# Retention, feed-forward and who issues the output stores: from SyncE to ScalarE, one unit later

## The chip, the cores and the metric

The kernel runs on one core of a Trainium2 chip. The metric is the device time of one execution in microseconds (us). The engines are TensorE (PE in the profile; PEld is its weight load), VectorE (DVE), ScalarE (ACT), GpSimd (POOL) and SyncE (SP); each works through its own list of instructions in order. SP computes nothing here: it issues DMAs. Engines wait for each other, and for DMAs, through semaphores.

## The reference

There are 8 batches of 8 heads, with 576 positions and a head dimension of 64. The first part is a retention layer: scores without a softmax, weighted by a power of a decay that each head has of its own. Its output is laid out as 4608 tokens of 512 values, and goes through a feed-forward layer of width 2048 with a sigmoid-approximated Gelu.

```python
scores = q @ k.T / sqrt(64)                       # each batch and head, 576 x 576
Dmat   = gamma[h] ** (i - j) if i >= j else 0     # gamma[h] = 1 - 2 ** (-5 - h)
ret    = (scores * Dmat) @ v                      # 576 x 64
x      = ret.transpose(0, 2, 1, 3).reshape(4608, 512)
h      = x @ w_in                                 # 512 -> 2048
out    = (h * sigmoid(1.702 * h)) @ w_out         # 2048 -> 512, float32
```

## The kernel before

**Two streams in one order.** The feed-forward layer is done in nine *chunks* of 512 tokens. `hidden` (L723) is one *unit* of its first half: four matmuls of 128x512 into a PSUM bank, and on ACT the Gelu from the bank to `gT` (L734). `project` (L759) is a unit of its second half: four of the sixteen matmuls that make 128 output rows. A chunk has four such *rows*, r = 0 to 3, of four units each (g = 0 to 3); rows 0 to 2 run interleaved, and row 3 after them (in chunk 0 all four are interleaved; chunk 1 is done in two halves, with rows 0 and 1 after the first and rows 2 and 3 after the second). When g is 3 a row is complete: ACT (in the last chunk DVE) copies the bank into one of three buffers `osb` (L771, L774), and SP issues the store to the output (L777, 256 KB). The buffer is chosen by a counter of the rows modulo 3.

Between these units lie the *steps* of retention for the later batches (`step`, `burst`): short 64x64 matmuls (L596 to L638), with DVE for masks, sums and the copy into `xT`. Which step comes behind which unit is written out by hand, in dictionaries that `run` (L953) reads. All of the units' banks come from three that take turns (`next_bank`), so a unit's matmuls wait until ACT has emptied the bank of three units ago.

**Transfers.** POOL issues the loads of q, k and v, three batches ahead, with at most a few in flight. SP issues the DMA transposes (`turn_dma`, L530) that turn the loaded q and k into `qk`, and, in the same list, the stores. SP's list follows the order in which the program was written down.

**Waits.** `Rec` records every operation and works out its waits: a reader waits for the last writer of a tile, a writer for the readers, DMAs among them. An engine waits for its own earlier operations too, except on PE and SP. A copy into an `osb` buffer thus waits for the landing of the store that last read this buffer.

**`later`.** This list holds operations that are recorded after the next unit. In the kernel before it holds only casts that ACT does for some of the steps (L717): `run` empties it behind each unit.

```python
unit(ahead)
while later:
    later.pop(0)()
```

The functions that the change touches, and what calls them:

Of the kernel before, what the change touches and what calls it, by code (L numbers as in the profile page):

```python
# [131 lines left out]
def bass_retnet_parallel__then__act_gelu_quick_kernel(  # L132
# [9 lines left out]
    R = Rec()  # L142
    es = ExitStack()
    with es:
        def sb(name, shape, dtype):
            return es.enter_context(nc.sbuf_tensor(name, shape, dtype))
# [33 lines left out]
        osb = [sb(f"osb{i}", [P, 512], FP32) for i in range(3)]  # L180
# [392 lines left out]
        def needs(m_out, m_in):  # L573
            r = []
            if m_out is not None:
                b, cs = chunks(m_out)
                r += [("sm", si(m_out)), "zw"] + [("v", b % NST, c) for c in cs] + queries(m_out)
            if m_in is not None:
                b, cs = chunks(m_in)
                r += [(nm, b % NST, c) for nm in "kv" for c in cs]  # L580
                r += [("qk", (NC * b + c) % NQK, 1) for c in cs] + queries(m_in)
            return r
# [113 lines left out]
        later = []  # L696
# [62 lines left out]
        def project(c, r, g, bank, key, eng="DVE", ahead=()):  # L759
            def fn(e):  # L760
                for f in range(4 * g, 4 * g + 4):
                    i = e.matmul(bank, gT[c % 2][:, f, 128 * r : 128 * r + 128], w_out_sb[:, f, :],  # L762
                                 start=(f == 0), stop=(f == NF - 1))
                return i
            R.op("PE", fn, r=[("w_out", g)] + [("gT", c % 2, f) for f in range(4 * g, 4 * g + 4)]
                 + list(ahead), ps=[key])
            if g == 3:
                m = ocount[0] % 3
                ocount[0] += 1
                if eng == "ACT":  # L770
                    R.op("ACT", lambda e: e.activation(osb[m].ap(), bank, AF.Copy),  # L771
                         w=[("osb", m)], ps=[key])
                else:
                    R.op("DVE", lambda e: e.tensor_copy(osb[m].ap(), bank),  # L774
                         w=[("osb", m)], ps=[key])
                row0 = 512 * c + 128 * r
                R.op("SP", lambda e: e.dma_start(out[row0 : row0 + 128, :], osb[m].ap()),  # L777
                     r=[("osb", m)], dma=("osb", m))

        def project_pieces(c, r, banks):  # L780

# [171 lines left out]
        def run(units, between):  # L953
            for i, unit in enumerate(units):
                ahead = []
                for fn, *args in between.get(i, ()):
                    if fn is step:
                        ahead += needs(args[0], args[0] + 1 if (len(args) < 2 or args[1])
                                       and args[0] + 1 < NWIDE else None)
                unit(ahead)  # L960
                while later:
                    later.pop(0)()
                for fn, *args in between.get(i, ()):
                    fn(*args)

# [7 lines left out]
        def units_o(c, rows, eng="ACT"):  # L973
            banks = {}

            def unit(r, g):
                def go(ahead):
                    if g == 0:
                        banks[r] = next_bank()
                    project(c, r, g, *banks[r], eng=eng, ahead=ahead)  # L980
                return go
            first = rows[:3]
            return ([unit(r, g) for g in range(4) for r in first]
                    + [unit(r, g) for r in rows[3:] for g in range(4)])

        first = {r: next_bank() for r in (1, 2, 3)}
        first[0] = wide_banks[3]
        run([lambda ahead, r=r, g=g: project(0, r, g, *first[r], eng="ACT", ahead=ahead)
             for g in range(4) for r in range(4)],
            {1: [(tail_turn,)], 3: [(intra, 4)], 5: [(turn, 5), (tail_out,), (regroup, 2)],  # L990
             7: [(scale_v, 5), (turn, 6)], 8: [(scale_v, 6), (regroup, 3)], 9: [(burst, None, 0, "ACT")],
             12: [(turn, 7)], 13: [(step, 0, False)], 14: [(scale_v, 7)], 15: [(turn, 8)]})
        turn_step(3)
        turn_step(4)
        run(units_half(1, 0),
            {0: [(turn, 9, True), (scale_v, 8), (scale_v, 9)], 1: [(burst, None, 1, "ACT")],
             5: [(step, 1)]})
        run(units_o(1, (0, 1)), {3: [(scale, 3)], 5: [(step, 2, False)]})
        run(units_half(1, 1), {2: [(burst, None, 3, "ACT")], 4: [(scale, 4)]})
        run(units_o(1, (2, 3)), {0: [(step, 3, True, "ACT")], 5: [(step, 4, False)], 6: [(scale, 5)]})  # L1000
# [19 lines left out]
        for r in range(3):  # L1020
            bank = next_bank()
            for g in range(4):
                project(NCH - 1, r, g, *bank)
# [59 lines left out]
```

## Time and profile before

| | |
|---|---|
| time, median of 3 runs | 300.65 us (299.34 to 302.87) |
| the profiled execution: its time | 299.83 us |
| its span in the profile | 298.0 us |
| PE busy | 290.4 us, 97% of the span |
| ACT busy | 125.8 us, 42% |
| DVE busy | 123.2 us, 41% |
| POOL busy (issue of loads) | 151.2 us, 51% |
| output stores issued by SP | 35 of 256 KB, one of 192 KB, one of 64 KB |
| DMA transposes issued by SP | 60 |
| time from issue to landing, median | store of 256 KB 3.6 us; transposes 7.3 and 7.4 us |

The profile shows one execution. The span is the time from its first instruction to its last; the execution's own time is 1.8 us longer. Busy time is what an engine spent on instructions, without those that only issue DMAs or wait. A wait is put down to the event that came last by the profile; where the engine named had long been done, it was another. "L771" is a line of the kernel.

### The profile page before, as it was taken

The page shows a single profiled execution, that of the slowest core. Times are in us where ns is not written, and L with a number is a line of the kernel's source. Part 1 is how long each engine was busy: PE and PEld are TensorE (multiplying, and loading weights), DVE is VectorE, ACT ScalarE, POOL GpSimd, SP SyncE. Part 2 cuts the span into 40 slices and gives each one's busy share as a digit, 9 for nine tenths or more (in the row PEclk, how much of TensorE's full clock was granted, in tenths as well). Part 3 has the DMA queues.
Part 4 walks back from the last instruction along what each step waited for, and adds up shares of the span by engine and source line. Part 5 has one row for each costly group of instructions (what it writes and reads, how often), then busy time and mean ns, then how long its engine had stood idle before and what let it go on. Part 6 is the DMA issues. An engine that isn't in the chain of part 4 may idle for free.

```text
span 298.0 us, 7691 instructions
## 1 busy us (share of the span) xinstructions
PE 290.4 (97%) x3396; PEld 148.2 (50%) x3396; DVE 123.2 (41%) x221; ACT 125.8 (42%) x208; POOL 151.2 (51%) x204
## 2 busy tenths in 40 slices
PE   7799999999899999999999999999999999999996
PEld 2554456848445444544454444444444444444444
DVE  6879375544435445533506223255226504000012
ACT  6667327617146413550365046503660265026600
POOL 8967969988959777568986896000000000000000
PEclk9999999999999999999999999999999999999999
DMA  9999999999999999999999999904820200030012
GB/s 131 166 194 186 170 171 165 169 137 139 188 142 129 175 155 168 178 127 137 164 213 137 119 186 180 62 2 107 162 46 2 108 35 2 0 108 35 0 47 96
DMA packets 154322, 36.04 MB, mean 121 GB/s; under 512 B 145456, under 2 KB 149808, under 8 KB 154288
## 3 DMA queue, kind: packets, MB, share of 16 engines
q0 software_dynamic: 115776, 18.10, 97.6%
q1 hardware_dynamic: 38512, 17.44, 31.9%
q8 instruction: 27, 0.44, 0.6%
q14 instruction: 7, 0.06, 0.1%
HBM read 36.70 MB, written 9.44 MB: 155 GB/s over the span
## 4 chain that ended last, share of the span: by engine, by line
PE 76%; DMA 10%; POOL 8%; DVE 4%; issue 1%; SPq 0%
PE psH L762 22%; PE psH L729 22%; PE psU L762 12%; PE psU L729 11%; DMA st_q<-in_q_dram 4%; POOL st_k L229 3%; POOL st_v L229 3%; DMA st_k<-in_k_dram 3%; DMA qk<-st_k 2%; PE psA L624 2%; POOL st_q L216 2%; DMA gT<-in_v_dram 2%; PE psA L596 1%; PE psA L638 1%; PE psA L612 1%; PE psA L788 1%
## 5 line engine op out<-in xcount | busy, mean ns | idle before, releaser
L762 PE MATMUL psH<-w_out_sb,gT 128*128 128x512 bf16 x352 | 84.1, 379 | 0.0
L729 PE MATMUL psH<-xT,w_in_sb 128*128 128x512 bf16 x328 | 78.5, 379 | 0.0
L682 DVE TENSOR_TENSOR xT<-psA,gq 128x768 bf16<-128x768 f32 x21 | 20.1, 958 | 117.3 <-PE psA L612 117.3
L734 ACT ACTIVATE gT<-psH 128x512 bf16<-128x512 f32 x82 | 48.8, 597 | 26.1 <-PE psH L729 26.0
L229 POOL DMA_DIRECT2D st_k<-in_k_dram x70 | 52.4, 774 | 13.8 <-DMA st_k<-in_k_dram 9.4
L229 POOL DMA_DIRECT2D st_v<-in_v_dram x70 | 52.1, 770 | 7.4 <-DMA st_v<-in_v_dram 3.5
L762 PEld LDWEIGHTS psH<-w_out_sb,gT 128*128 128x128 bf16 x352 | 33.6, 98 | 39.3 <-DVE sm L693 0.2
L729 PEld LDWEIGHTS psH<-xT,w_in_sb 128*128 128x128 bf16 x328 | 31.7, 98 | 37.7 <-ACT gT L846 0.3
L762 PE MATMUL psU<-w_out_sb,gT 128*128 128x512 bf16 x192 | 47.9, 379 | 1.3 <-DMA qk<-st_k 1.3
L729 PE MATMUL psU<-xT,w_in_sb 128*128 128x512 bf16 x164 | 42.1, 379 | 0.0
L216 POOL DMA_DIRECT2D st_q<-in_q_dram x39 | 35.1, 901 | 10.2 <-DMA st_q<-in_q_dram 8.6
L771 ACT ACTIVATE osb<-psH 128x512 f32<-128x512 f32 x20 | 11.9, 597 | 58.5 <-PE psH L762 58.5
L734 ACT ACTIVATE gT<-psU 128x512 bf16<-128x512 f32 x41 | 24.5, 598 | 12.2 <-PE psU L729 12.2
L762 PEld LDWEIGHTS psU<-w_out_sb,gT 128*128 128x128 bf16 x192 | 18.1, 98 | 22.4 <-issue 1.6
L729 PEld LDWEIGHTS psU<-xT,w_in_sb 128*128 128x128 bf16 x164 | 15.7, 98 | 18.8 <-ACT osb L771 0.3
L387 DVE TENSOR_TENSOR st_v<-st_v,vfac 128x512 bf16<-128x512 bf16 x36 | 23.4, 683 | 3.5 <-DMA st_v<-in_v_dram 3.5
L711 DVE TENSOR_TENSOR zacc<-zacc,psA 128x256 f32<-128x256 f32 x49 | 20.5, 418 | 5.5 <-PE psA L624 4.2
L771 ACT ACTIVATE osb<-psU 128x512 f32<-128x512 f32 x11 | 6.6, 597 | 32.0 <-PE psU L762 28.3
L693 DVE TENSOR_TENSOR sm<-psA,maskw 128x768 bf16<-128x768 f32 x21 | 19.9, 948 | 0.0
L596 PE MATMUL psA<-sm,st_v 64*64 64x64 bf16 x504 | 11.7, 195 | 0.3
L746 PE MATMUL psH<-xT,w_in_sb 128*128 128x256 bf16 x96 | 11.8, 273 | 0.0
L624 PE MATMUL psA<-st_v,st_k 64*64 64x64 bf16 x448 | 11.7, 199 | 0.0
(118 smaller groups left out, 217.9 us busy)
## 6 DMA issues: line engine op xcount, KB each, us to landing
out_dram<-osb SPq DMA_DIRECT2D x35, 256.0 KB, 3.6
st_q<-in_q_dram POOLq DMA_DIRECT2D x31, 128.0 KB, 7.4
st_k<-in_k_dram POOLq DMA_DIRECT2D x57, 64.0 KB, 7.4
st_v<-in_v_dram POOLq DMA_DIRECT2D x57, 64.0 KB, 7.4
w_in_sb<-in_moe_w_in_dram POOLq DMA_DIRECT2D x4, 512.0 KB, 7.5
w_out_sb<-in_moe_w_out_dram POOLq DMA_DIRECT2D x4, 512.0 KB, 11.7
st_k<-in_k_dram POOLq DMA_DIRECT2D x4, 128.0 KB, 4.6
st_q<-in_q_dram POOLq DMA_DIRECT2D x8, 64.0 KB, 7.2
```

The costliest lines, as they stand in the source:

```text
L216: paced(R.op("POOL", lambda e, d=d, s=s: e.dma_start(d, s), w=[(nm, sl, c)], dma=(nm, sl, c), own=pace()))
L229: paced(R.op("POOL", lambda e: [e.dma_start(d, s) for d, s in parts], w=[(nm, sl, c)], dma=(nm, sl, c), parts=2, own=pace()))
L387: R.op(eng, lambda e: e.tensor_tensor(t, t, f, ALU.mult), r=[("vfac", min(b, 1))], w=[("v", sl, c)])
L596: i = e.matmul(psA[half(t), 2 + u, at : at + 64], rows_of(st_v, m_out, g, u, 4 * u + 2 * t + j), smw[si(m_out)][half(r), j, 2 * blk + t, : ...
L624: i = e.matmul(psA[half(j), bank, off + 64 * t : off + 64 * t + 64], rows_of(st_k, m_in, g, u, h), rows_of(st_v, m_in, g, u, h), start=(t ...
L682: R.op("DVE", lambda e: e.tensor_tensor(xT[:, :, t0 : t0 + 192].rearrange("p (u j) n -> p u j n", u=2), psA[:, 2:4, 0:384].rearrange("p u ...
L693: R.op("DVE", lambda e: e.tensor_tensor(o, i, k, ALU.mult), r=["maskw"], w=[("sm", si(m))], ps=["S"])
L711: R.op("DVE", lambda e, to=to, src=src, was=was: e.tensor_tensor(to, was, src, ALU.add), r=[("zacc", (blk - 1) % 3)], w=[("zacc", blk)], p ...
L729: i = e.matmul(bank, w_in_sb[:, a, 128 * f : 128 * f + 128], xT[:, a, 512 * c : 512 * c + 512], start=(a == 0), stop=(a == 3))
L734: R.op("ACT", lambda e: e.activation(gT[c % 2][:, f, :], bank, AF.Gelu_apprx_sigmoid), w=[("gT", c % 2, f)], ps=[key])
L762: i = e.matmul(bank, gT[c % 2][:, f, 128 * r : 128 * r + 128], w_out_sb[:, f, :], start=(f == 0), stop=(f == NF - 1))
L771: R.op("ACT", lambda e: e.activation(osb[m].ap(), bank, AF.Copy), w=[("osb", m)], ps=[key])
```

## The change

ScalarE issues the store of each row that it copied. The store is not recorded at once but put into `later`, and `run` now takes what was in the list *before* the unit and records it behind the unit: a store follows its copy by one unit. (The casts in the list keep their places, since they are put there between units.) The rows of the last chunk, which DVE copies, are stored by SP as before. SP's list keeps the 60 transposes, the two loads of the start and the five stores of the last chunk.

```diff
                 row0 = 512 * c + 128 * r
-                R.op("SP", lambda e: e.dma_start(out[row0 : row0 + 128, :], osb[m].ap()),
-                     r=[("osb", m)], dma=("osb", m))
+
+                def store(by):
+                    R.op(by, lambda e: e.dma_start(out[row0 : row0 + 128, :], osb[m].ap()),
+                         r=[("osb", m)], dma=("osb", m))
+                if eng == "ACT":
+                    later.append(lambda: store("ACT"))
+                else:
+                    store("SP")
...
+                due = list(later)
+                later.clear()
                 unit(ahead)
-                while later:
-                    later.pop(0)()
+                for fn in due:
+                    fn()
                 for fn, *args in between.get(i, ()):
                     fn(*args)
```

In ACT's list the order at the end of a usual chunk becomes: copy of row 0, copy of row 1, store of row 0, copy of row 2, stores of rows 1 and 2, copy of row 3; then the first Gelu of the next chunk, the store of row 3, and the second Gelu. In SP's list the transposes stand behind each other, and 21 of them have a wait for PE added (that the `qk` buffer has been read), which the stores ahead of them had implied.

## The prediction

> **What bounds the kernel now.** I read the page's table of engines first, then its slices, then the waits of TensorE (PE).
>
> ```profile
> span 298.0 us, 7691 instructions
> ...
> PE 290.4 (97%) x3396; PEld 148.2 (50%) x3396; DVE 123.2 (41%) x221; ACT 125.8 (42%) x208; POOL 151.2 (51%) x204
> ...
> PEclk9999999999999999999999999999999999999999
> ```
>
> PE is busy for 290.4 of 298.0 us at a full granted clock, and no other engine is near it. The list of waits, asked for PE alone from 20 us to the end, has one row:
>
> ```profile
> engine line waited for: us in total, times, longest us
> PE psU L762 <- DMA qk<-st_k: 1.3, 1, 1.3
> ```
>
> So after the start-up there is one visible wait of 1.3 us. That is nearly all that a better order of stores could win; a loss has no such limit. The chain from 60 to 78 us tells where it comes from:
>
> ```profile
> 60.46 7.99 DMA st_k<-in_k_dram
> 68.45 0.02 issue
> 68.46 7.38 DMA qk<-st_k
> 75.84 0.24 issue
> 76.09 1.02 PE psU L762 x4
> ```
>
> A load of K lands at 68.45, SP then issues a transpose of it, this lands at 75.84, and PE goes on. The transpose waited for the load, not for a store ahead of it on SP.
>
> **What the change removes.** SP loses 32 of its 37 stores (the copies of L771: 20 + 11 + 1). One takes SP 333 ns (median of L777; 332 to 1145), 10.7 us in all. SP also waited 138.5 us at these stores for the copies (the waits of SP: L777 <- ACT osb L771), with transposes queued behind. Those are issued earlier now, as soon as their loads are there and PE has read the old contents of their buffers. Gain: nothing, since PE waits for a transpose once and that one waited for its load. The bounds are 0 and the 1.3 us of that wait.
>
> **What it adds: issue time on ScalarE (ACT).** 32 x 0.333 = 10.7 us, and ACT's busy time goes from 125.8 to about 136.5 us. What hides it? The place with work close behind a store is the start of a chunk, where the last row's store follows the first Gelu (ACT's timeline, then PE's: start us, us, engine, line, operation, idle before it and what ended that):
>
> ```profile
> 207.80 0.60 ACT L771 ACTIVATE osb<-psU 128x512 f32<-128x512 f32 x1 [2.86 <-PE psU L762]
> 208.66 0.60 ACT L734 ACTIVATE gT<-psH 128x512 bf16<-128x512 f32 x1 [0.27 <-PE psH L729]
> 209.53 0.60 ACT L734 ACTIVATE gT<-psH 128x512 bf16<-128x512 f32 x1 [0.27 <-PE psH L729]
> ```
>
> ```profile
> 210.19 1.89 PE L729 MATMUL psH<-xT,w_in_sb 128*128 128x512 bf16 x8
> ```
>
> Three banks take turns. The Gelu at 209.53 ends at 210.13 and PE needs its bank one unit (0.86 us) after 210.19, at 211.05: 0.92 us spare. With the 0.27 us that ACT idles ahead of it, a store may take 1.19 us before PE notices. The median is 0.33 and the longest of L777 1.145, so I cost this at nothing. Without that cover a store costs what it takes beyond 1.19 us: if it also had to sit out SP's longest transpose issue (2.64 us, L530), 2.64 + 0.33 - 1.19 = 1.8 us, at nine places (row 3 of seven full chunks, and two of chunk 1, done in halves). A store's wait for its own copy is on the same engine a unit back: nothing.
>
> **What it moves: the store of row 0 comes later, and row 3 needs its buffer.** There are three osb buffers and four rows, so the copy of a chunk's row 3 must wait until the store of row 0 has landed; ACT runs in order, so it now stands there with the Gelus behind it. SP issued that store right behind the copy. ACT issues it behind the *copy of row 1*. The kernel before already shows the wait in chunk 2 (again ACT's timeline, then PE's):
>
> ```profile
> 110.32 0.60 ACT L771 ACTIVATE osb<-psU 128x512 f32<-128x512 f32 x1 [9.03 <-PE psU L762]
> 111.19 0.60 ACT L771 ACTIVATE osb<-psH 128x512 f32<-128x512 f32 x1 [0.27 <-PE psH L762]
> ...
> 117.37 0.60 ACT L771 ACTIVATE osb<-psU 128x512 f32<-128x512 f32 x1 [3.73 <-PE psH L729]
> ```
>
> ```profile
> 118.03 1.03 PE L729 MATMUL psU<-xT,w_in_sb 128*128 128x512 bf16 x4
> ```
>
> PE had finished row 3 by 116.30, so its copy could have started near 116.5. It starts at 117.37, and the wait is put down to a PE that had long been done; row 0's store, issued at 110.94 with 6.3 us to landing (L777 in that window), lands at 117.3. The copy ends at 117.97 and PE takes that psU bank at 118.03: 0.06 us spare. Now chunk by chunk:
>
> - Chunk 2: issue after 111.19 + 0.60 = 111.79. The store that SP issued at 111.8 took 6.5 us, so landing is 118.3, the copy ends at 118.9 and PE waits 118.9 - 118.03 = 0.9 us. Bounds: 0 (landing no later than 117.3, if transposes that moved forward leave the queues freer) and 1.8 (the longest landing of L777, 7.5 us).
> - Chunk 0: copies of rows 0, 1 and 3 start at 45.91, 47.30 and 49.76. Issue moves from 46.53 to 47.90; the store at 47.9 took 3.3 us, landing 51.2, so row 3 is copied 1.4 us late. Its bank is wanted at 51.33 and the copy then ends at 51.8: 0.5 us, and as ACT is packed until 53 us the qk evacuation and Gelus behind are late too. I take 1.0 us (0.5 to 1.5). This delay lies ahead of PE's 1.34 us wait at 74.5 to 76.1, whose end a load sets, so it is absorbed there: 0 at the end, and its full size if that cover goes.
> - Chunk 3: copies at 141.15, 143.01 and 147.33. Issue goes from 141.77 to 143.61; landing took 3.7 us at 141.8 and 5.7 at 146.2. That gives 147.3 to 149.3, and PE needs the bank at 148.85: 0 to 1.1. Midway the copy ends at 148.9, so 0.1.
> - Chunk 4: the store at 173.4 took 3.9 us, landing 177.3 against a copy at 177.11, 0.2 late with 0.9 to spare: 0. From chunk 5 landings are near 2.2 us and issues come at least 3.7 us ahead: 0. Chunk 1 works in halves and its stores now go some 7 us earlier: 0.
>
> **What collides.** Rows 0 and 1 of chunk 1 are copied at 66.25 and 67.11, but SP stored them at 74.6 and 75.2, behind its transposes. ACT will store them near 68, beside the transpose of 68.46 that PE waits for. How much of the DMA engines is a store? From 262 to 272 us four stores run alone:
>
> ```profile
> q1 hardware_dynamic: 576, 1.05, 28.9%
> ```
>
> 28.9% of 10 us over four is 0.72 us of all 16 engines each, 1.44 for two. Bounds of the delay: 0 and 1.44; I take the middle, 0.7. The Trainium skill, page "DMA: Bandwidth & Descriptors", section "Issuing engines are not separate DMA queues", says that DMAs from any engine interleave on the same 16 DMA engines, and that spreading the issue saves only sequencer time. By that rule the term is towards 1.44 and the freed SP brings nothing. No row here has two issuers of that queue.
>
> **The sum.** 0.7 + 0.9 + 0.1 = 1.7 us. The profiled execution took 299.83 us (span 298.0 and 1.8 around it), so 301.5. The median of the runs, 300.65, lies 0.8 above that execution; on it the sum is 302.3. I predict halfway, 301.9.
>
> **The rivals.**
>
> 1. *Slower: ACT's stores queue behind SP's transposes.* Place: the nine stores with Gelus close behind. If a store must sit out a transpose issue, the median (1.27 us for K) costs 1.27 + 0.33 - 1.19 = 0.4 us, the longest 1.8. It decides from a held store of 1.19 us. Nine at 0.4 is 3.6 on top of 301.9: 305.5; half of them 303.7. For: SP's stores among transposes took up to 1.145 us instead of 0.33, and transposes hold SP for some 80 us (60 x 1.3). Against: after 110 us transposes should follow a step and be past before row 3's store. The Trainium skill, page "Perfetto Trace Analysis", section "DMA Instruction — HWDGE (DVE, Sync)", says that the descriptor generator is shared by sequencers and locked while one uses it, and that the profiled time holds the wait for that lock. No row of this trace has two of them at it.
> 2. *Nothing on the path.* Landings are shorter because stores no longer sit among late transposes, and the stores near 68 us pass beside the transpose: 299.8 to 300.65, say 300.3. For: light stages land in 2.2 us. Against: the landings around 111 us are 6.3 and 6.5 with loads still running.
> 3. *Faster: the wait at 76 us goes,* because stores leave SP's queue and later transposes no longer follow them: 299.83 - 1.3 = 298.5. Against: the chain shows a load ahead of that transpose.
>
> **How the numbers follow.** Forecast (held copies, some collision) 0.50; rival 1 0.22; rival 2 0.20; rival 3 0.08. The range 299.2 to 305.0 takes the forecast's bounds (up to 1.44 + 1.8 + 1.1 at once is 304.2 on the profiled execution), most of rival 1 and all of rival 2, and leaves out rival 3 and the far end of rival 1. About what a measurement here tells from no change is 1%, 3.0 us: 297.6 to 303.7 round the median. Rival 3 ends inside; faster gets 0.04, for a gain that I don't see. Slower gets most of rival 1 and the top of the forecast, 0.25. Same: 0.71.
>
> **What would show it.** Right: ACT's copies of row 3 in chunks 0 and 2 start near 51.2 and 118.3 (plus the shift by then), after the landing of row 0's store and not after PE; PE shows new waits of about 0.5 to 1 us there; the wait at 76 us ends later than 75.84 + 0.24; stores on ACT take 0.33 to 1.15 us. Wrong: row 3's copies follow PE by the usual 0.2 us; stores on ACT of 2 us and more with PE waiting for Gelus (rival 1); PE's wait at 76 us gone (rival 3); or a span that changes by over 3 us with no wait at these places.

## The result, and the profile after

| | before | changed |
|---|---|---|
| time, median of 6 runs | 300.41 us (298.99 to 302.87) | 304.52 us (301.76 to 306.74) |
| ratio, with its 95% interval | | 1.0109 (1.0066 to 1.0152) |
| the profiled execution: its time, its span | 299.83, 298.0 us | 304.51, 302.6 us |

The changed kernel is slower by 1.1%, some 3.3 us. Here and below a ratio leaves out executions that lie over 1.5% above the fastest of their kernel, and a median holds all of them, so the two can differ.

The page of the changed kernel, its lines for engines and clock:

```profile
span 302.6 us, 7719 instructions
...
PE 291.7 (96%) x3396; PEld 148.7 (49%) x3396; DVE 122.7 (41%) x221; ACT 125.5 (41%) x208; POOL 151.5 (50%) x204
...
PEclk9999999999999999999999997999999999999999
```

PE has the same 3396 matmuls and is busy for little longer, but the span is 4.6 us longer, and one slice has a lower clock. The waits of PE from 20 us on have again a single row, a new one:

```profile
engine line waited for: us in total, times, longest us
PE psH L729 <- ACT osb L771: 3.2, 1, 3.2
```

The row of before, the wait for a transpose near 76 us, is gone. In its place PE waits 3.2 us for ScalarE's copy of an output row. The chain from 170 to 187 us follows it back (start us, us, what):

```profile
170.65 1.74 PE psH L762 x8
172.39 0.02 issue
172.42 0.01 ACT osb L771
172.42 8.44 DMA out_dram<-osb
...
180.95 0.61 ACT osb L771
181.56 0.05 issue
181.60 2.52 PE psH L729 x8
```

This is the end of chunk 4. ACT issues row 0's store at 172.42; it takes 8.44 us to land; only then may ACT copy row 3 into the same buffer; only then has PE its bank. ACT's timeline names the wait itself (the bracket is the idle time ahead and what ended it), then PE's:

```profile
171.55 0.60 ACT L771 ACTIVATE osb<-psH 128x512 f32<-128x512 f32 x1 [9.03 <-PE psH L762]
172.42 0.60 ACT L771 ACTIVATE osb<-psH 128x512 f32<-128x512 f32 x1 [0.27 <-PE psH L762]
172.42 0.34 ACTq L779 DMA_DIRECT2D out_dram<-osb  x1
...
180.95 0.60 ACT L771 ACTIVATE osb<-psH 128x512 f32<-128x512 f32 x1 [7.07 <-DMA out_dram<-osb]
```

```profile
177.40 1.03 PE L729 MATMUL psU<-xT,w_in_sb 128*128 128x512 bf16 x4
181.60 2.52 PE L729 MATMUL psH<-xT,w_in_sb 128*128 128x512 bf16 x8 [3.18 <-ACT osb L771]
```

Before, the same store was issued at 172.6 and landed in 3.3 us. The windows of the stall and of what follows it (busy us and instruction counts of PE, PEld, DVE, ACT and POOL, then the granted clock, the DMA share and GB/s):

```profile
178.00:182.00 4.00, 0.82 (x4) 0.21 (x3) 0.00 (x0) 1.05 (x3) 2.75 (x4) 1.00 1.43 241
182.00:187.00 5.00, 5.00 (x33) 1.82 (x35) 0.00 (x0) 2.40 (x6) 0.00 (x0) 0.66 1.70 151
```

After the wait the granted clock is 0.66 over 5 us: 5 x 0.34 = 1.7 us more. So 3.2 + 1.7 = 4.9 us against a difference of 4.7 us between the two profiled executions. PE's lost wait of 1.3 us at 76 us was little gain: PE came to this point 1.0 us later, after a wait of 1.4 us at 16 us (`psA L846 <- DVE sm`), ahead of every store, and went on at 75.61 us instead of 76.09.

What changed for the DMAs is in SP's timeline. Before, SP stood at the stores of chunk 4 from 158.8 us on, and the next nine transposes were issued between 178 and 205 us. Now they go out from 156 to 172 us, the last of them 0.2 us ahead of row 0's store:

```profile
168.23 1.19 SPq L530 DMA_TRANSPOSE qk<-st_k  x1
169.52 1.21 SPq L530 DMA_TRANSPOSE qk<-st_q  x1
172.22 1.90 SPq L530 DMA_TRANSPOSE qk<-st_k  x1
```

### The profile page after: what moved, and what is told of

It reads as the page before. It is cut to its first block, busy times and chain, and to the rows that moved or that the text cites. A ratio compares the mean times of both kernels' runs of the same rounds, so it can differ in the third digit from the quotient of the medians.

```text
span 302.6 us, 7719 instructions
## 1 busy us (share of the span) xinstructions
PE 291.7 (96%) x3396; PEld 148.7 (49%) x3396; DVE 122.7 (41%) x221; ACT 125.5 (41%) x208; POOL 151.5 (50%) x204
## 4 chain that ended last, share of the span: by engine, by line
PE 92%; DMA 4%; DVE 1%; POOL 1%; issue 1%; ACT 0%; POOLq 0%; ACTq 0%
PE psH L762 24%; PE psH L729 24%; PE psU L762 14%; PE psU L729 12%; PE psH L746 4%; DMA out_dram<-osb 3%; PE psA L624 2%; PE psA L596 2%; PE psA L638 2%; DMA st_k<-in_k_dram 1%; PE psA L612 1%; PE psU L746 1%; PE psA L762 1%; PE psA L794 1%; PE psA L408 1%; DVE sm L438 1%
## 5 line engine op out<-in xcount | busy, mean ns | idle before, releaser
L729 PE MATMUL psH<-xT,w_in_sb 128*128 128x512 bf16 x328 | 79.4, 382 | 3.2 <-ACT osb L771 3.2
L729 PE MATMUL psU<-xT,w_in_sb 128*128 128x512 bf16 x164 | 43.0, 385 | 0.0
```

Source lines behind the costliest of these rows:

```text
L729: i = e.matmul(bank, w_in_sb[:, a, 128 * f : 128 * f + 128], xT[:, a, 512 * c : 512 * c + 512], start=(a == 0), stop=(a == 3))
```

## The experiments

Theory A: row 3's copy is held on ACT until row 0's store has landed, and this landing is longer because transposes that SP's stores held back run beside it. Rivals: the issue of stores on ACT delays the Gelus (B), chance (C), the third queue alone makes stores land late (D), the delay by one unit alone (E). "Free" means transposes as in the changed kernel; "held" means that they wait for the copies again.

| kernel | median us | ratio to before |
|---|---|---|
| changed: free, 3 buffers | 304.52; again 303.01 | 1.0109 (1.0066 to 1.0152); again 1.0103 (1.0018 to 1.0188) |
| changed, 4 buffers | 301.58; again 301.07 | 1.0034 (1.0003 to 1.0065); again 1.0035 (1.0005 to 1.0064) |
| before, 4 buffers | 300.05 | 0.9998 (0.9960 to 1.0036) |
| changed, held | 300.92 | 1.0017 (0.9985 to 1.0049) |
| changed, row 0 stored by SP | 300.99 | 1.0020 (0.9987 to 1.0053) |
| changed, nine transposes held | 304.94 | 1.0052 (0.9981 to 1.0123) |
| changed, store right behind copy | 303.27 | 1.0080 (1.0028 to 1.0133) |
| changed, 4 buffers, two stores a row | 302.39 | 1.0023 (0.9975 to 1.0070) |
| changed, stores two units behind | 307.57 | 1.0222 (1.0160 to 1.0284) |
| changed, 4 buffers, held | 300.64 | 1.0012 (0.9983 to 1.0041) |

**Four buffers.**

```diff
-        osb = [sb(f"osb{i}", [P, 512], FP32) for i in range(3)]
+        osb = [sb(f"osb{i}", [P, 512], FP32) for i in range(4)]
...
-                m = ocount[0] % 3
+                m = ocount[0] % 4
```

> The changed kernel with four osb buffers, so that the copy of row 3 no longer waits for the store of row 0. Theory A (row 3's copy is held on ScalarE until row 0's store has landed, which takes longer because the transposes are no longer held back; TensorE then idles 3.2 us and runs 3.4 us at half clock): no wait of ScalarE for out_dram<-osb, no wait of TensorE for osb, no slice of lower clock, and about 304.5 - 3.3 - 1.7 = 299.5 us (299 to 300.8). Theory B (the stores' issue on ScalarE delays the Gelus): the issues are all still there, so 303 to 305. Theory C (run to run differences alone): 300 to 305 with the spread of the changed kernel.

The store of chunk 4's row 0 again took long, 7.6 us from 174.8, but row 3 no longer waited for it. ACT's timeline of this run:

```profile
174.82 0.38 ACTq L779 DMA_DIRECT2D out_dram<-osb  x1
...
179.12 0.60 ACT L771 ACTIVATE osb<-psH 128x512 f32<-128x512 f32 x1 [2.86 <-PE psH L762]
```

The copy follows PE, PE has no wait after 20 us, and the ratio falls from 1.0109 to 1.0034. So the hold on the buffer is most of the loss. The lower clock did not quite go: this profile has it at the start, after a wait of 1.8 us for `w_in` near 16 us, ahead of all stores. Executions of the kernel before have a lower mean clock too (0.994 in 8 of the 25 that ran beside the second set of experiments), though no trace of one tells where.

> The kernel before with four osb buffers, the control to the run above. Theory A: TensorE never waited for a copy of row 3 there, so 300.4 us as before (299.3 to 301.5); only ScalarE's late copy of row 3 in chunk 2 (117.37 instead of about 116.5) comes earlier. Theory B: the same. If a fourth buffer itself were worth something, it would be below 299.

It came out so: 0.9998. The fourth buffer by itself makes no difference that can be told.

**Transposes held again.** `copied[0]` is the last copy that ACT was given.

```diff
-                    r=[(nm, sl, c)], w=[("qk", n % NQK, a)], dma=("turn", n % NQK, a))
+                    r=[(nm, sl, c)], w=[("qk", n % NQK, a)], dma=("turn", n % NQK, a),
+                    own=copied[0])
```

> The changed kernel, three buffers, stores on ScalarE, but every transpose waits for the last copied row, as it did behind the stores on SyncE. Theory A, its part on the transposes: row 0's store of chunk 4 lands in 3 to 5 us instead of 8.4, TensorE waits for osb 0 to 0.5 us, 299.8 to 301.5 us. Rival D (stores land late because ScalarE's queue shares the DMA engines with two others, whatever the transposes do): landing stays near 8 us, the wait of 3 us stays, 303 to 305.

Row 0's store of chunk 4, from ACT's queue, landed in 2.8 us, and row 3's copy came on time (line numbers are three higher here):

```profile
172.92 0.34 ACTq L782 DMA_DIRECT2D out_dram<-osb  x1
...
177.23 0.60 ACT L774 ACTIVATE osb<-psH 128x512 f32<-128x512 f32 x1 [2.86 <-PE psH L765]
```

Three buffers, 32 stores on ACT and one unit of delay are all still there, and the ratio is 1.0017, no difference that can be told. That is against B, D and E. ACT still waits 8.2 us for landings in three other chunks, and none of it reaches PE.

What the DMA engines did while the store was under way shows in the DMA view of 170 to 184 us (what the engines moved, in 40 slices of 0.35 us), first of the changed kernel, then of the held one:

```profile
GB/s 148 198 162 147 149 213 188 146 6 1 9 10 130 150 150 193 209 166 145 149 158 177 209 189 194 271 225 215 316 334 321 279 179 151 149 155 152 149 151 149
...
GB/s 100 66 15 54 84 148 144 123 77 98 101 218 317 286 217 341 325 167 143 240 289 261 209 160 147 151 134 127 148 176 181 202 245 294 218 140 146 153 140 161
```

In the changed kernel the engines move 10 GB/s or less for four slices, 172.8 to 174.2 us, just after the store was issued, and then about 150; the held kernel has no such hole behind its issue at 172.9. All six profiles with free transposes and at most one unit of delay have one of 0.5 to 1.4 us here, within 1 us of the issue. The kernel before, the three profiles with these transposes held and the one with two units of delay have none there. Elsewhere such holes come in the kernel before too (136.6 to 137.9 us); what makes them is not shown.

**Row 0 by SP.** `if eng == "ACT" and r > 0:` in place of `if eng == "ACT":` ahead of `later.append`.

> The changed kernel, three buffers, but row 0 of each chunk is stored by SyncE right behind its copy; rows 1 to 3 stay on ScalarE. Theory A: only row 0's store has a copy waiting for it, and it again goes out ahead of the transposes behind it: landing 3 to 5 us in chunk 4, no stall over 0.5 us, 299.8 to 301.5. Theory B: the stores with Gelus close behind (row 3) are still on ScalarE, so 303 to 305. Rival D: row 0 is on SyncE's queue, so landing is short: as theory A.

1.0020: no difference that can be told, with 24 stores still on ACT, among them all that have Gelus close behind. Chunk 4's row 3 was copied as soon as PE was done with it. This too holds the transposes, since SP waits for row 0's copy.

**Only nine transposes held.** The edit of above, with `own=copied[0] if hold[0] else None`, and `hold[0]` set in chunk 5's region alone.

> The changed kernel, three buffers, with only the transposes that are recorded in chunk 5's region held for the last copied row (the nine that moved from 178-205 us to 156-172 us are held, the 44 ahead of them run as early as in the changed kernel). Theory A: they are what lengthened the landing of chunk 4's row 0 from 3.3 to 8.4 us; landing 3 to 5 us there, no stall over 0.5 us, no half clock, 299.8 to 301.5 us. If any earlier transpose, or the loads alone, did it: landing 7 to 8.5 us and 303 to 305.

Half of it came true. In chunk 4 the landing was 3.0 us and no wait was left; but the median stayed at 304.94 us, and the interval of the ratio, 0.9981 to 1.0123, decides nothing. The waits of PE in the profiled execution, which took 305.83 us:

```profile
PE psU L732 <- ACT osb L774: 1.6, 1, 1.6
PE psH L765 <- issue: 0.9, 1, 0.9
PE psH L732 <- ACT osb L774: 0.8, 1, 0.8
```

Now chunks 2 and 3 wait for their copies of row 3, with landings of 7.9 and 6.0 us. These chunks run as in the changed kernel, whose first profile showed 5.3 and 4.9 us there. So chunk 4 is one place among three, and which one hurts differs between executions.

**The store right behind its copy**, without `later`.

> The changed kernel with each store on ScalarE right behind its own copy instead of one unit later; three buffers, transposes free. Theory A with the free transposes as the cause: issue comes only 0.2 to 1.2 us earlier (0.2 in chunk 4), landing there stays 7 to 8.5 us, TensorE waits 2.5 to 3.3 us and drops to half clock: 303 to 305. Rival E (the delay by one unit is the cause): the stall goes, 300 to 301.5.

Inconclusive in the profile, as chunk 4's landing was near 5 us (issue 174.41, row 3's copy 179.56) and PE waited only 0.4 us, in chunk 2. In the times the loss is there: 1.0080. To give up the unit of delay does not cure it, so E is not the cause; how much the delay adds is open here.

**Two stores a row.** Four buffers, and each store as two of half the columns: 64 issues.

> The changed kernel with four buffers, each row stored in two halves, so 64 issues on ScalarE instead of 32. Theory B (issue time on ScalarE reaches TensorE): the rest of 1 us that four buffers left over the kernel before doubles: 302.5 to 303.5. Theory A: two issues take 0.68 us, less than the 1.19 us that are free, so 301.6 as with one (300 to 302).

1.0023 against 1.0034: twice the issues cost nothing that can be told, though the interval, 0.9975 to 1.0070, leaves room for another 1 us. The median, 302.39 us, lies between the two forecasts. They do reach PE where ACT is packed, near 55 and 73 us:

```profile
PE psU L746 <- ACT qk L415: 0.5, 1, 0.5
PE psH L746 <- ACT gT L752: 0.4, 1, 0.4
```

The wait of 76 us lies behind these and is gone in this profile; PE goes on there at 77.05 us, 1.0 us later than in the kernel before, so it can have taken in only a part of them and of a wait of 1.4 us at the start. With one issue a row no such wait shows.

**The changed kernel again.**

> The changed kernel once more, for a second profile and more times. Theory A: the stall at chunk 4's row 3 is in every execution, since all earlier runs show a lower mean clock: TensorE waits 1.5 to 3.5 us for osb near 178 us, 302 to 305 us. Rival C (chance): a profile without that stall, or with it in another chunk, and times that reach below 301.

1.0103, as before, but spread otherwise: in this profile PE waits for copies of row 3 twice, 1.6 us in all, in chunks 3 and 4, behind landings of 6.2 and 5.9 us. The granted clock stayed at 1.00 after both; the lower clock of this profile lies at the start. There were only four executions. "In every execution near 178 us for 1.5 to 3.5 us" was too narrow.

**Two units behind.** The stores go through a second list first.

```diff
-                    later.append(lambda: store("ACT"))
+                    stage.append(lambda: store("ACT"))
...
-                later.clear()
+                later[:] = stage
+                stage.clear()
```

> The changed kernel with each store two units behind its copy instead of one; three buffers, transposes free. Theory A (row 3's copy is held until row 0's store has landed): row 0 is stored behind the copy of row 2, 1.9 us later in chunk 2 and 0.9 us later in chunks 3 and 4, so TensorE's waits for osb there grow by about as much each: 2 to 3.5 us on top of the 303 to 304.5 of the changed kernel, 305 to 308 us. From chunk 5 on nothing, since over 2 us were spare. Rivals B and C (issue time, or chance): 302 to 305 as the changed kernel.

307.57 us, 1.0222, from four executions. In the profiled execution, of 310.68 us, the delay reaches PE three times, in chunks 2, 3 and 0:

```profile
PE psU L729 <- ACT osb L771: 2.5, 1, 2.5
PE psH L729 <- ACT osb L771: 2.3, 1, 2.3
PE psH L746 <- ACT osb L771: 2.0, 1, 2.0
```

An issue that is later by 0.9 to 1.9 us buys waits of that order, as theory A says, and B and C don't. Chunk 4 was spared: its row 3 was copied at 188.38, 3.8 us after the issue of row 0's store, which landed in 3.7 us although two transposes had been issued 3.2 and 4.4 us ahead of it.

**The rest of 0.3%.**

> The changed kernel with four buffers once more, in five rounds: is the rest of 0.3% real? Theory A has no copy left to hold, so a rest must come from the free transposes or from the stores' issue: if it is only noise, a ratio of 0.998 to 1.002; if real, 1.003 to 1.006, and then the next run tells which.

> Four buffers, stores on ScalarE, and the transposes held for the last copied row as on SyncE before. If the rest of the run above comes from the free transposes: 0.998 to 1.001 of the kernel before. If it comes from the stores' issue on ScalarE: as the run above.

1.0035 again, so a rest of about 1 us is real; with held transposes it is 1.0012. This points to the free transposes, but the two intervals overlap, so where the rest comes from stays open. The clock may have a part: a mean clock of 0.994 or less is in 9 of the 22 executions with four buffers and in 14 of the 79 of the kernel before. At 1.7 us each that is some 0.4 us, an estimate, and whether the change or chance makes it more frequent is not shown. No version beat the kernel before.

**Row 0's landing in all profiles.** The time from issue to landing of row 0's store, us, by chunk. "Free" are the profiles with one store a row and at most one unit of delay; chunk 4 of the run with nine transposes held counts as held:

| transposes | chunk 2 | chunk 3 | chunk 4 |
|---|---|---|---|
| kernel before, 3 and 4 buffers | 6.3, 6.8 | 3.7, 5.2 | 3.3, 3.3 |
| free | 5.2 to 7.9 (six) | 4.9 to 6.3 (six) | 5.1 to 8.4 (five) |
| held | 5.1, 6.0 | 3.6, at most 5.1 | 2.8, 3.0, 3.4 |

That free transposes lengthen the landing is clear in chunk 4 and likely in chunk 3. In chunk 2 the ranges overlap: there the landing was long before the change too, and a part of the free transposes in it is not shown.

## Why the prediction was right or wrong

**The time.** 304.52 us lies in the range (299.2 to 305.0); 301.9 was 2.6 us low. On the ratio the loss is 3.3 us where 1.7 was summed. That the range held it is in part luck: its top came from rival 1 and from the bounds of the collision and of chunks 2 and 3 added up, and the first profile lost nothing at any of these. By the prediction's own line for no change (up to 303.7) the result is slower, to which it gave 0.25.

**What bounds the kernel** was read rightly: PE, with one wait to win and no limit to what could be lost.

**"The store of row 0 comes later, and row 3 needs its buffer"** is the mechanism; four buffers take most of the loss away. Its terms were mis-sized. Chunk 2 was put at 0.9, chunk 3 at 0.1 and chunk 4 at 0; the first profile shows 0, 0 and 3.2 us, the second 0, 0.9 and 0.6. The sign that row 3's copies in chunks 0 and 2 follow the landing came true (50.86 and 116.39 us, both put down to `DMA out_dram<-osb`), but PE waited at neither; and a sign of being wrong came true as well: a span longer by over 3 us with no wait of PE at these two places. Two steps failed:

- *Issue time.* I let row 0's store wait for the end of row 1's copy. ACT issues it as that copy starts: in chunk 2 at 110.96 with the copy at 110.95, against 110.94 on SP before. Counted from the end of row 0's copy, that is 0.28 us instead of 0.02, so 0.26 us later where I took 0.85; and the landing, 5.3 us, was even shorter.
- *Landing time.* I took it from stores that SP had issued. For chunk 4 I took 3.9 us and called row 3's copy "0.2 late with 0.9 to spare". But in chunk 4 this store landed fast *because* SP's list kept the transposes behind it. Under "What the change removes" I saw that transposes would be issued earlier, costed it by what PE could win, and did not ask what they would then run beside. With transposes free this store took 8.4, 7.6, 5.9, 5.2 and 5.1 us (3.7 with two units of delay); held, 2.8, 3.0 and 3.4.

**The clock** was not in the sum. The wait of 3.2 us brought 1.7 us more; those of 0.9 and 0.6 us in the second profile brought none.

**Chunk 0** was put at 1.0 us, absorbed at 76 us. In the first profile row 3's copy there was about 0.2 us late (landing 2.6 us, the copy at 50.86, PE done with the row at 50.64), PE did not wait, and there was nothing to absorb. The wait that was to absorb it ran from 74.75 us, not from 74.5.

**"What collides"**, 0.7 us, was not seen. In the changed kernel the transpose in question was issued at 67.7 and landed in 7.6 us, where it had taken 7.4; with held transposes PE waited 1.0 us there instead of 1.3.

**ACT's issue time at nothing** was right: 0.34 us at the median and 1.24 at most, no wait of PE for it, and doubling the issues changed nothing that can be told. (The profile's page does not count issues as busy time, so ACT's 125.8 us became 125.5, not 136.5.) With it rival 1 falls as a cause, though its mechanism shows faintly: four of the 32 stores took longer than 0.39 us, 0.53 to 1.24, each during or right behind a transpose's issue on SP (85.69 us, 1.24 us, beside a transpose of 85.36 to 87.00). Other stores inside such issues took 0.34 to 0.39 us, so no store had to sit out a whole one. The Trainium skill (page "Perfetto Trace Analysis", section "DMA Instruction — HWDGE (DVE, Sync)") would allow a wait for a shared generator; whether these four are that, no row tells.

**Rival 2** (nothing on the path) is what the held kernel does, at 1.0017; in the changed one chunk 4's landings did not get shorter but longer. **Rival 3**'s sign, the wait at 76 us gone, was there with little of its gain: PE was 1.0 us late already, and went on 0.5 us earlier than before.

## What to carry to other kernels

A queue that issues in order is also a fence: before moving part of its list elsewhere, list what stood behind the moved part, when it will be issued now, and which transfers it will then run beside. With three buffers and four rows, the time from issue to landing is on the path of an in-order engine wherever it exceeds the distance to the next use, so price it with the queues as they will be and not as they were. Spare room of a us or less is a warning even where nothing waits yet: chunk 4's, put at 0.9 us, was the one that failed.

## What the runs showed of the hardware

**The granted clock falls after a wait of PE of 2 to 3 us, but not always.** In the kernel with stores two units behind, the windows that follow the waits of 2.0, 2.5 and 2.3 us:

```profile
56.00:61.00 5.00, 5.00 (x75) 3.80 (x75) 2.13 (x4) 3.69 (x6) 5.00 (x8) 0.66 2.02 177
...
124.80:129.80 5.00, 5.00 (x16) 1.91 (x16) 0.00 (x0) 2.63 (x5) 2.38 (x4) 0.66 1.96 138
...
159.80:164.80 5.00, 4.94 (x23) 2.27 (x24) 0.00 (x0) 3.78 (x8) 1.37 (x2) 1.00 1.85 140
```

Two of the three cost another 1.7 us, as the 3.2 us in the changed kernel did; the 1.3 us of the kernel before cost nothing more. The Trainium skill (page "TensorE: Matmul & The Clock Gate", section "Part 1: The HAM clock gate") says that the clock drops to half after at least one idle window of about 3.4 us. That there is a drop to half agrees: in the changed kernel the granted clock is 0.50 from 183 to 186 us. Here waits of 2.0, 2.5 and 3.2 us were enough.

**A store of 256 KB lands in 2.0 to 8.7 us** in the changed kernel's first profile: 2.0 us at 208.15 and 238.84, where the engines are mostly idle, and 8.7 us at 85.69, among loads and transposes. The share of the DMA engines that it takes, 0.72 us, says little about that.
